# Retention and two feed-forward layers on one core: joining steps, stores, loads and one add put in another order

## The chip, the cores and the metric

The kernel runs on one core of a Trainium2 chip. The metric is the device time of one execution in microseconds. TensorE (PE in the rows) multiplies; VectorE (DVE), ScalarE (ACT) and GpSimd (POOL) do the element work; SyncE (SP) issues nearly all DMAs. The median of three runs is given, and a further execution was profiled.

## The reference

The input is q, k, v in float32, 4 batches of 8 heads, 576 positions, 64 wide, and the weights of two feed-forward layers. What is computed, in float32:

```python
scores = scale * q @ k.T                       # scale = 1/sqrt(64)
ret    = scores * Dmat                         # gamma_h ** (i - j) for i >= j, else 0
x      = (ret @ v), heads side by side         # 2304 x 512
x      = max(x @ w1, x @ w2, x @ w3) @ w_out   # 512 -> 768 -> 512
g, val = x @ w_gate, x @ w_val                 # 512 -> 1536
out    = (g * sigmoid(g) * val) @ w_out2       # 2304 x 512
```

## The kernel before

To keep float32 accuracy a factor is split into two halves (h and l), and a product takes three multiplications: l by h, h by l, h by h. The weights come from memory as 64-bit words (w64) and are joined to float32 by the *joining steps*: ScalarE scales the two words (L115, L121), VectorE shifts and merges them (L123, L124: "wz") and adds (L126: "wl"), ScalarE and GpSimd then split the result (L134 wh, L136 wlo). The order of every engine's instructions is written out by hand: an engine runs its instructions in the order of the program text, so the order of the text is the order of the work.

*Visits.* The retention has 32 units (a pair of heads and half the positions); `visit(n, ...)` handles one: the product with the state and the values (`a_value`, L285 to L292, whose second half xl is L294), the loads for a later unit (`a_load` for kn, vn, L167; `t_load` for qk, eight DMAs at L188), the next state (`a_state`, st, L274), the next scores (`a_score`, pT, L250), and then 4 to 6 *slices* of the first layer. A slice (`f_slice`, L341) is twelve products into one of two PSUM buffers (tag "mm") and one evacuation: for w1 ScalarE copies (L355), for w2 and w3 VectorE takes the maximum (L357). Slices go w1, w2, w3 for each block of 128 hidden columns, each for two halves of 288 tokens (h0, h1). When a maximum is done (w3) it is stored to memory (h_d, L359) by SP. There are three buffers for maxima, so the copy for w1, h1 of a block reuses the buffer of h0 of the block before, and waits for that store to land.

Within a visit the joining steps are divided into shares, one before each slice (L383 to L388). Before unit 16 they join the weights of the first layer; from visit 16 on, `early_steps` (L439) does the same for the second layer's weights: load 512 KB, join, store 256 KB to l_d (L447).

*Remaining slices*, 262 to 339 us: the rest of the first layer; w_out is joined beside it.

*Output stage*, 339 to 417 us (L684): the maxima are loaded back (`h_load`, hf, L524, six buffers, four loads ahead), split (`h_split`, L530 hh on ScalarE, L531 hl), and multiplied with w_out (L698); ScalarE copies the result (L708, "B") and `xsteps` form the operands of the next stage. Beside it `split_parts` (L591) splits the second layer's weights of block 1 and stores them (w_d1, L599), and `split` those of block 0.

*Groups*, from 417 us (L755, index j): the second layer by a scheme with seven products (T1 to T4, B11, B21, B22) in three PSUM buffers g1 to g3. In a group, u (L785) empties g2 before the product "d, T3" may start, p (L797) before "b, T4" may. The add L790 for p5 is on GpSimd, behind GpSimd's gl (L817) of the group before. Between the products `hook()` issues a step of the weights' preparation (`w_steps`, L612 to L627, which need loads of l_d, L431) or of `xsteps`. How many is `pace`.

SP's DMAs land in the order in which they were issued. An instruction that issues a DMA and has to wait holds those behind it on SP.

Of the kernel before, what the change touches and what calls it, by code (L numbers as in the profile page):

```python
# [16 lines left out]
ALU = mybir.AluOpType  # L17
# [51 lines left out]
def retention_moe(ctx, tc, consts, q, k, v, w1, w2, w3, w_out, w_gate, w_val, w_out2, out):  # L69
# [259 lines left out]
    def conv_plan(convs):  # L329

        for _ in range(convs):
            i = wc[0]
            if i < len(win_units):
                wc[0] += 1
                yield (i, 2), (i + 1, 0)
                yield (i, 3), (i + 1, 1)
                yield (i, 4), (i, 5)

    mx = {}

    def f_slice(hb, fi, wi):  # L341
        assert win_units.index((fi, wi)) in ready
        wh, wl = w_in[(fi, wi)]
        cw = TOK[hb][1]
        ps = ps_mm.tile([P, C], F32, name="ps", tag="mm")[:, 0:cw]
        n = 0
        for kc in range(KD):
            xh, xl = xs[(hb, kc)]
            ksl = slice(kc * P, kc * P + P)
            for l, r in ((wh, xl), (wl, xh), (wh, xh)):  # L350
                pe.matmul(ps, l[:, ksl], r, start=n == 0, stop=n == 3 * KD - 1)  # L351
                n += 1
        if wi == 0:
            mx[hb] = ffn.tile([P, C], F32, name="hmax", tag="hmax", bufs=3)[:, 0:cw]
            act.activation(mx[hb], ps, ACTF.Copy)  # L355
        else:
            dve.tensor_tensor(mx[hb], ps, mx[hb], ALU.max)  # L357
        if wi == 2:
            sp.dma_start(out=h_d[hb][fi], in_=mx[hb])  # L359

    fq = []

# [10 lines left out]
            pe.matmul(ps, zero[:, 0:P], zero, start=True, stop=True)  # L373

    def visit(n, slices, convs):
        low = a_value(n)
        if n % 2:
            a_load(n // 2 + 3)
        else:
            t_load(n // 2 + 2)  # L380
        if n % (2 * NP) == 2 * NP - 1:
            fq.extend((n // NP - 1 + h, *w) for w in win_units for h in range(2))
        a_state(n + 1)  # L383
        low()
        a_score(n + 1)
        plan = list(conv_plan(convs))
        done = 0
        for j in range(slices + 1):  # L388
            if j == min(2, slices - 1) or not slices:
                a_prep(n + 2)  # L390
            upto = len(plan) * (j + 1) // (slices + 1)
            for step in plan[done:upto]:
                for i, ph in step:
                    win_phase(i, ph)
            done = upto
            if n >= 16:
                for _ in range(1 if j % 2 else 2):
                    next(early, None)
            if j < slices:
                f_some(1)  # L400

# [134 lines left out]
    for j in range(len(fq) + 1):  # L536
        f_some(1)
        next(steps, None)
        if j % 3 == 0:
            next(steps, None)  # L540
        x = j - late
        if x >= 0 and x % 2 == 0 and x // 2 < F1:
            h_load(0, x // 2)
        if x >= 4 and x % 2 == 0 and (x - 4) // 2 < F1:
            h_split(0, (x - 4) // 2)
    for _ in steps:
        pass
    for fi in range(F1 - 2, F1):
# [42 lines left out]
    def split_parts(fi, nm, src):  # L591

        w = dict(WOPS)[nm]
        for c0 in range(0, w, 256):
            t = xf.tile([P, 2, HT], F32R, name="xt", tag="xt", bufs=3)[:, :, 0:256]
            act.activation(t[:, 0], src[:, c0:c0 + 256], ACTF.Copy)
            yield
            dve.tensor_tensor(t[:, 1], src[:, c0:c0 + 256], f(t[:, 0]), ALU.subtract)
            sp.dma_start(out=w_d[(fi, nm)][:, :, c0:c0 + 256], in_=f(t))  # L599
            yield  # L600

    def w_steps(fis, split=split):

# [75 lines left out]
    xsteps = iter(())  # L679
    NHX = 2 * NBK  # L680
    hq = [(hx, fi) for hx in range(1, NHX) for fi in range(F1)]
    for x in hq[:4]:
        h_load(*x)
    for hx in range(NHX):  # L684
        b, half = divmod(hx, 2)
        if half == 0:
            r = {}
            if b < NBK - 1:
                x_open(b)
        for e in range(KD):  # L690
            ps = ps_mm.tile([P, 512], F32, name="ps2", tag="mm")
            n = 0
            for fi in range(F1):
                wh, wl = wo[fi]
                hh, hl = hsp[(hx, fi)]
                es = slice(e * P, e * P + P)
                for l, rr in ((wh, hl), (wl, hh), (wh, hh)):
                    pe.matmul(ps[:, 0:HT], l[:, es], rr, start=n == 0, stop=n == 3 * F1 - 1)  # L698
                    n += 1
            for fi in ((0, 1), (2,), (), (3, 4, 5))[e]:  # L700
                if hx + 1 < NHX:
                    h_split(*hq.pop(0))
                    if len(hq) > 3:
                        h_load(*hq[3])
            nm = RAW[(e // 2, half)]
            if nm not in r:
                r[nm] = raw(nm)
            act.activation(r[nm][:, e % 2], ps[:, 0:HT], ACTF.Copy)  # L708
            for _ in range(4 if e < 2 else 3):
                next(xsteps, None)  # L710
            if half or hx == 0:
                for _ in range(3):
                    next(steps, None)
        for _ in xsteps:
            pass
        xsteps = (x_second if half else x_first)(b, r)
# [38 lines left out]
    def group(fi, b, hook, lastg=False):  # L755
        X = xop[b]
        g1, g2, g3 = [psg.tile([P, HT], F32, name=f"g{i}", tag=f"g{i}") for i in range(3)]

        def tmp(nm, bufs=1):
            return gw.tile([P, HT], F32, name=nm, tag=nm, bufs=bufs)  # L760

        def prod(ps, w, off, x, first):
            t = wop[(fi, w)]
            xh, xl = X[x]
            n = 0
            for kc in range(2):
                ks = slice(off + kc * P, off + kc * P + P)
                for l, r in ((t[:, 0], xl), (t[:, 1], xh), (t[:, 0], xh)):
                    pe.matmul(ps, l[:, ks], r[:, kc], start=first and n == 0, stop=n == 5, skip_group_check=True)  # L769
                    n += 1  # L770

        def o():
            if pend:
                out2(*pend.pop(0))
            hook()

        prod(g1, "a", 0, "B11", True)
        p1 = tmp("p1", 2)
        act.activation(p1, g1, ACTF.Copy)
        while held:  # L780
            held.pop()()
        hook()
        prod(g2, "c", 256, "T2", True)
        u2 = tmp("u2")
        dve.tensor_tensor(u2, g2, p1, ALU.add)  # L785
        hook()
        prod(g3, "c", 0, "T1", True)
        p5 = tmp("p5", 2)
        act.activation(p5, g3, ACTF.Copy)
        pool.tensor_tensor(p5, p1, p5, ALU.add)  # L790
        hook()
        prod(g1, "a", 256, "B21", False)
        sa = tmp("sa")
        act.activation(sa, g1, ACTF.Sigmoid)
        hook()
        prod(g2, "d", 0, "T3", False)
        dve.tensor_tensor(p5, g2, p5, ALU.add)  # L797
        dve.tensor_tensor(sa, g1, sa, ALU.mult)
        hook()
        o()  # L800
        o()
        prod(g3, "d", 256, "B22", False)
        dve.tensor_tensor(u2, g3, u2, ALU.add)  # L803
        sb = tmp("sb")
        act.activation(sb, u2, ACTF.Sigmoid)  # L805
        hook()
        if not lastg:
            o()
        gh, gl = {}, {}
        for half in (1, 0):  # L810
            for y, t in (("gh", gh), ("gl", gl)):
                t[half] = gw.tile([P, HT], F32R, name=y, tag=y, bufs=8)
            gs[(fi, b, half)] = (gh[half], gl[half])

        def fin(half, t):
            act.activation(gh[half], t, ACTF.Copy)  # L816
            pool.tensor_tensor(gl[half], t, f(gh[half]), ALU.subtract)  # L817

        dve.tensor_tensor(u2, u2, sb, ALU.mult)
        dve.tensor_tensor(p5, u2, p5, ALU.mult)  # L820
        prod(g2, "b", 0, "T4", False)
        fin(1, p5)
        dve.tensor_tensor(p1, g2, p1, ALU.add)
        dve.tensor_tensor(p1, sa, p1, ALU.mult)
        held.append(lambda: fin(0, p1))
        if lastg:
            held.pop()()
        hook()
        if lastg:
            o()  # L830
        if fi % GRP == GRP - 1:
            pend.extend((fi // GRP, b, half, s) for half in (1, 0) for s in range(ROWS))
# [5 lines left out]
    for j, (fi, b) in enumerate(seq):  # L838
# [11 lines left out]
        if (fi, b) == (F2 - 1, 0):  # L850
            for _ in steps:
                pass
        pace = 0 if j == 2 else 2 if j == 3 or fi == F2 - 2 and b == 0 else 1

        def hook():
            beat[0] += 1
            if j < 3 and beat[0] % 2:
                next(xsteps, None)
            for _ in range(pace):
                next(steps, None)  # L860
# [41 lines left out]
```

## Time and profile before

| | us |
|---|---|
| median of three runs | 841.12 (841.1 to 842.18) |
| profiled execution | 842.47 |
| its span, first to last instruction | 840.7 |
| TensorE busy | 816.8 (97%) |
| VectorE busy | 563.0 (67%) |
| ScalarE busy | 315.3 (38%) |
| GpSimd busy | 209.5 (25%) |
| DMA queue of SP, share of 16 engines | 57.4% |
| granted TensorE clock, mean | 1.000 |

An engine's busy time overlaps with that of the others. A number in brackets behind an instruction, such as [2.22 <-DVE hmax L357], is the idle time before it and what ended that. Line numbers in rows are those of the kernel before.

### The profile page before, as it was taken

What the parts mean: (1) busy time and instruction counts of PE and PEld (TensorE: products, weight loads), DVE (VectorE), ACT (ScalarE), POOL (GpSimd) and SP (SyncE); (2) the same over time, 40 slices, a digit from 0 to 9 for tenths busy, and PEclk for the clock granted to TensorE, in tenths of its full rate; (3) what the DMA queues carried; (4) which work ended last, traced back from release to release, by engine and by line L of the source; (5) the groups of instructions that cost most, each with busy time, mean ns of one, the idle gap of its engine ahead of it and who ended that gap; (6) DMA issues with size and microseconds to landing.
All of it is one profiled execution on the core that took longest, in us unless ns stands there. A gap on an engine that the chain in (4) does not pass through costs nothing.

```text
span 840.7 us, 15502 instructions
## 1 busy us (share of the span) xinstructions
PE 816.8 (97%) x5925; PEld 762.4 (91%) x5933; DVE 563.0 (67%) x1004; ACT 315.3 (38%) x633; POOL 209.5 (25%) x197
## 2 busy tenths in 40 slices
PE   8898999999999999999999999999999999999998
PEld 6798888999989999999988999999998999999996
DVE  2668866777775345367578788988989555545555
ACT  2545513333331133446444553444334222332220
POOL 4233430000000002224043223333323333223331
PEclk9999999999999999999999999999999999999999
DMA  9999639999983133675355443443340616665532
GB/s 179 231 208 218 148 73 240 254 245 254 236 233 115 39 127 103 202 210 177 112 233 215 163 153 134 152 150 137 130 149 13 263 39 226 237 217 207 198 105 75
DMA packets 165801, 142.94 MB, mean 170 GB/s; under 512 B 101344, under 2 KB 137952, under 8 KB 165728
## 3 DMA queue, kind: packets, MB, share of 16 engines
q1 hardware_dynamic: 164368, 141.56, 57.4%
q8 instruction: 46, 0.75, 0.4%
q10 hardware_dynamic: 1360, 0.41, 0.2%
q14 instruction: 27, 0.22, 0.1%
HBM read 93.70 MB, written 48.23 MB: 169 GB/s over the span
## 4 chain that ended last, share of the span: by engine, by line
PE 58%; issue 16%; DVE 9%; POOL 7%; DMA 5%; ACT 2%; SPq 2%; POOLq 0%; DVEq 0%; ACTq 0%
PE ps L351 20%; PE g L769 17%; PE ps L746 11%; POOL gl L817 4%; PE ps L698 4%; POOL p L790 2%; PE o_ps L289 2%; PE s L248 2%; DVE wz L124 1%; PE o_ps L285 1%; DMA h_d<-hmax 1%; SPq L188 1%; POOL hl L531 1%; DVE wl L126 1%; DVE wz L123 1%
## 5 line engine op out<-in xcount | busy, mean ns | idle before, releaser
L351 PE MATMUL ps<-xl,wh 128*128 128x288 f32 x576 | 173.5, 301 | 8.7 <-DVE hmax L357 6.4
L351 PE MATMUL ps<-xh,wh 128*128 128x288 f32 x576 | 169.7, 295 | 0.0
L351 PE MATMUL ps<-xh,wlo 128*128 128x288 f32 x576 | 169.6, 294 | 0.0
L817 POOL TENSOR_TENSOR gl<-p,gh 128x384 fp32r<-128x384 f32 x72 | 85.0, 1198 | 275.8 <-ACT gh L816 275.8
L746 PE MATMUL ps<-wp,gh 128*128 128x512 f32 (+1 forms) x436 | 135.3, 391 | 0.4 <-DVE acc L751 0.3
L351 PEld LDWEIGHTS ps<-xl,wh 128*128 128x128 f32 x576 | 108.0, 188 | 13.7 <-DVE hmax L357 6.8
L351 PEld LDWEIGHTS ps<-xh,wlo 128*128 128x128 f32 x576 | 108.1, 188 | 0.0
L351 PEld LDWEIGHTS ps<-xh,wh 128*128 128x128 f32 x576 | 108.1, 188 | 0.0
L746 PEld LDWEIGHTS ps<-wp,gh 128*128 128x128 f32 x436 | 80.7, 188 | 14.4 <-DVE acc L751 1.0
L746 PE MATMUL ps<-wp,gl 128*128 128x512 f32 (+1 forms) x218 | 85.6, 393 | 0.0
L751 DVE TENSOR_TENSOR acc<-ps,acc 128x512 f32<-128x512 f32 (+1 forms) x91 | 62.2, 684 | 33.5 <-PE ps L746 32.3
L357 DVE TENSOR_TENSOR hmax<-ps,hmax 128x288 f32<-128x288 f32 x96 | 43.5, 454 | 60.4 <-PE ps L351 52.4
L769 PE MATMUL g<-xhB,wa 128*128 128x384 f32 x288 | 73.4, 336 | 0.0
L769 PE MATMUL g<-xhT,wc 128*128 128x384 f32 x288 | 73.2, 335 | 0.0
L531 POOL TENSOR_TENSOR hl<-hf,hh 128x384 fp32r<-128x384 f32 x26 | 29.4, 1137 | 132.4 <-ACT hh L530 132.4
L805 ACT ACTIVATE sb<-u 128x384 f32<-128x384 f32 x36 | 18.9, 525 | 112.1 <-DVE u L803 112.1
L816 ACT ACTIVATE gh<-p 128x384 fp32r<-128x384 f32 x72 | 37.8, 525 | 60.8 <-DVE p L820 53.9
L218 POOL TENSOR_TENSOR ks<-kn,cst_a 96x384 f32<-96x384 f32 (+1 forms) x32 | 24.7, 775 | 129.7 <-PE m_ps L264 121.5
L797 DVE TENSOR_TENSOR p<-g,p 128x384 f32<-128x384 f32 x36 | 20.0, 554 | 49.6 <-PE g L769 42.3
L355 ACT ACTIVATE hmax<-ps 128x288 f32<-128x288 f32 x48 | 19.6, 411 | 89.2 <-PE ps L351 77.9
L769 PEld LDWEIGHTS g<-xhB,wa 128*128 128x128 f32 x288 | 52.1, 188 | 0.0
L769 PEld LDWEIGHTS g<-xhT,wc 128*128 128x128 f32 x288 | 52.0, 188 | 0.0
(118 smaller groups left out, 1711.6 us busy)
## 6 DMA issues: line engine op xcount, KB each, us to landing
w<-in_moe_w_out_dram SPq DMA_DIRECT2D x18, 512.0 KB, 4.2
w<-l_d SPq DMA_DIRECT2D x28, 256.0 KB, 3.6
h_d<-hmax SPq DMA_DIRECT2D x48, 144.0 KB, 2.5
w<-in_moe_w_dram SPq DMA_DIRECT2D x12, 512.0 KB, 6.6
w<-in_moe_w_gate_dram SPq DMA_DIRECT2D x12, 512.0 KB, 5.8
w<-in_moe_w_val_dram SPq DMA_DIRECT2D x12, 512.0 KB, 5.4
vn<-in_v_dram SPq DMA_DIRECT2D x16, 288.0 KB, 6.4
out_dram<-acc SPq DMA_DIRECT2D x17, 256.0 KB, 2.0
```

Of the source, the lines that this page charges most:

```text
L218: pool.tensor_tensor(u["ks"][:, 0:nk], u["k"][:, 0:nk], sc, ALU.mult)
L351: pe.matmul(ps, l[:, ksl], r, start=n == 0, stop=n == 3 * KD - 1)
L355: act.activation(mx[hb], ps, ACTF.Copy)
L357: dve.tensor_tensor(mx[hb], ps, mx[hb], ALU.max)
L531: (dve if fi in (3, 5) and hx else pool).tensor_tensor(hl, hf, f(hh), ALU.subtract)
L698: pe.matmul(ps[:, 0:HT], l[:, es], rr, start=n == 0, stop=n == 3 * F1 - 1)
L746: pe.matmul(ps[:, cs], l[:, sl], r[:, cs], start=n == 0, stop=n == 3 * GRP - 1)
L751: dve.tensor_tensor(a[:, cs], ps[:, cs], a[:, cs], ALU.add)
L769: pe.matmul(ps, l[:, ks], r[:, kc], start=first and n == 0, stop=n == 5, skip_group_check=True)
L797: dve.tensor_tensor(p5, g2, p5, ALU.add)
L816: act.activation(gh[half], t, ACTF.Copy)
L817: pool.tensor_tensor(gl[half], t, f(gh[half]), ALU.subtract)
```

## The change

1. In a visit with slices, the first share of joining steps (and, from visit 16 on, the first early steps) is issued right behind `a_value`, ahead of the loads, the state, xl and the scores.
2. A finished maximum is put on a list, and its store is issued at the start of the next slice (`store_mx`), or after the last slice.
3. In the output stage five loads of hf are asked for ahead, not four.
4. `split_parts` gives way once more before it issues a store.
5. The add for p5 is on VectorE for the first three groups, in which GpSimd has no gl that the output waits for.
6. In group 3, `pace` is 1 instead of 2, with one more step per hook from the sixth on; the count of hooks starts anew in each group, and the hooks at which a step of `xsteps` is issued alternate with j.

The code of the change (an instruction at line L of before stands at another line number in the rows of the order of after: L357 at L364, L359 at L345, L447 at L462, L612, L614, L617 at L628, L630, L633, L785 at L801, L790 at L806, L797 at L813, L824 at L840):

```diff
@@ slices @@
     mx = {}
+    done_mx = []
+
+    def store_mx():
+        while done_mx:
+            dst, t = done_mx.pop()
+            sp.dma_start(out=dst, in_=t)
 
     def f_slice(hb, fi, wi):
         assert win_units.index((fi, wi)) in ready
+        store_mx()
...
         if wi == 2:
-            sp.dma_start(out=h_d[hb][fi], in_=mx[hb])
+            done_mx.append((h_d[hb][fi], mx[hb]))
@@ visit @@
     def visit(n, slices, convs):
+        plan = list(conv_plan(convs))
+        done = 0
+
+        def share(j):
+            nonlocal done
+            upto = len(plan) * (j + 1) // (slices + 1)
+            for step in plan[done:upto]:
+                for i, ph in step:
+                    win_phase(i, ph)
+            done = upto
+            if n >= 16:
+                for _ in range(1 if j % 2 else 2):
+                    next(early, None)
+
         low = a_value(n)
+        if slices:
+            share(0)
         if n % 2:
             a_load(n // 2 + 3)
         else:
...
         for j in range(slices + 1):
             if j == min(2, slices - 1) or not slices:
                 a_prep(n + 2)
-            upto = len(plan) * (j + 1) // (slices + 1)
-            for step in plan[done:upto]:
-                for i, ph in step:
-                    win_phase(i, ph)
-            done = upto
-            if n >= 16:
-                for _ in range(1 if j % 2 else 2):
-                    next(early, None)
+            if j or not slices:
+                share(j)
@@ split_parts @@
             dve.tensor_tensor(t[:, 1], src[:, c0:c0 + 256], f(t[:, 0]), ALU.subtract)
+            yield
             sp.dma_start(out=w_d[(fi, nm)][:, :, c0:c0 + 256], in_=f(t))
-            yield
@@ output stage @@
-    for x in hq[:4]:
+    for x in hq[:5]:
         h_load(*x)
...
-                    if len(hq) > 3:
-                        h_load(*hq[3])
+                    if len(hq) > 4:
+                        h_load(*hq[4])
@@ groups @@
-        pool.tensor_tensor(p5, p1, p5, ALU.add)
+        (pool if pend or b == NBK - 1 or fi > 1 else dve).tensor_tensor(p5, p1, p5, ALU.add)
...
-        pace = 0 if j == 2 else 2 if j == 3 or fi == F2 - 2 and b == 0 else 1
+        pace = 0 if j == 2 else 2 if fi == F2 - 2 and b == 0 else 1
+        beat[0] = 0
 
         def hook():
             beat[0] += 1
-            if j < 3 and beat[0] % 2:
+            if j == 3 and beat[0] > 5:
+                next(steps, None)
+            if j < 3 and (beat[0] + j) % 2:
                 next(xsteps, None)
```

TensorE's instructions stand in the same order before and after. Three places show what moves on the other engines.

VectorE in the visit around 83 us; st is the state, xl the second half of the retention's result, pT the scores, hmax the maximum. Before:

```order
L126 ISA wl<-wz,wl 128x1024
L274 SCALAR_TENSOR_TENSOR st<-st,cst_a,m_ps 128x64 x2
L294 TENSOR_TENSOR xl<-o_ps,xh 128x288
L250 TENSOR_TENSOR pT<-s,dm_88 96x576
L123 TENSOR_SCALAR wz<-wz 128x512
L124 SCALAR_TENSOR_TENSOR wz<-w_1053,wz 128x512
L357 TENSOR_TENSOR hmax<-ps,hmax 128x288
```

After:

```order
L126 ISA wl<-wz,wl 128x1024
L123 TENSOR_SCALAR wz<-wz 128x512
L124 SCALAR_TENSOR_TENSOR wz<-w_1053,wz 128x512
L274 SCALAR_TENSOR_TENSOR st<-st,cst_a,m_ps 128x64 x2
L294 TENSOR_TENSOR xl<-o_ps,xh 128x288
L250 TENSOR_TENSOR pT<-s,dm_88 96x576
L364 TENSOR_TENSOR hmax<-ps,hmax 128x288
```

The two merging instructions of the joining moved from behind pT to ahead of the state; the maximum stands behind all of them in both.

SP near 200 us, in a visit of the saturated stretch: h_d are stores of maxima, kn and vn loads of the retention, w loads of weights (512 KB each), l_d stores of joined weights. Before:

```order
L447 DMA l_d_1_106<-w64e 128x512
L359 DMA h_d_59<-hmax 128x288
L167 DMA kn<-in_k_dram 96x12x64
L167 DMA vn<-in_v_dram 96x12x64
L106 DMA w_2865<-in_moe_w_val_dram 128x4x128
L359 DMA h_d_60<-hmax 128x288
L447 DMA l_d_0_107<-wl 128x512
```

After:

```order
L462 DMA l_d_1_106<-w64e 128x512
L106 DMA w_2839<-in_moe_w_val_dram 128x4x128
L167 DMA kn<-in_k_dram 96x12x64
L167 DMA vn<-in_v_dram 96x12x64
L345 DMA h_d_59<-hmax 128x288
L462 DMA l_d_0_107<-wl 128x512
L345 DMA h_d_60<-hmax 128x288
```

The weight load moved ahead of kn and vn, and the first store of a maximum behind all three loads; the second store also stands behind an l_d store now.

VectorE at the start of group j = 3: u and p of the last lines are those of the new group, L824 ends the group before. Before:

```order
L824 TENSOR_TENSOR p_5631<-sa,p_5631 128x384
L612 TENSOR_TENSOR wz<-w_5170 128x256
L614 TENSOR_TENSOR wz<-wz,w_5168 128x256
L785 TENSOR_TENSOR u_5733<-g_5710,p_5718 128x384
L617 TENSOR_TENSOR wz<-w_5168,w_5170 128x256
```

After:

```order
L840 TENSOR_TENSOR p_5631<-sa,p_5631 128x384
L628 TENSOR_TENSOR wz<-w_5173 128x256
L801 TENSOR_TENSOR u_5732<-g_5710,p_5718 128x384
L630 TENSOR_TENSOR wz<-wz,w_5171 128x256
L633 TENSOR_TENSOR wz<-w_5171,w_5173 128x256
```

L614 moved behind u; L612 stays ahead of it.

## Rows read from the trace of the kernel before

**Rows 1.** The page, first part: engine, busy us (share of the span), instructions.

```profile
PE 816.8 (97%) x5925; PEld 762.4 (91%) x5933; DVE 563.0 (67%) x1004; ACT 315.3 (38%) x633; POOL 209.5 (25%) x197
```

**Rows 2.** TensorE's waits: what waited, for what: us in total, times, longest.

```profile
PE ps L351 <- DVE hmax L357: 6.4, 7, 2.2
PE ps L351 <- ACT hmax L355: 2.2, 3, 1.1
PE g L769 <- DVE u L785: 2.0, 2, 1.6
PE g L769 <- DVE p L797: 1.7, 2, 0.9
...
PE ps L698 <- ACT B L708: 1.0, 1, 1.0
...
PE ps L698 <- DVE hl L531: 0.5, 2, 0.3
```

**Rows 3.** Windows: busy us of PE, PEld, DVE, ACT, POOL; clock, DMA share, GB/s.

```profile
140.00:160.00 20.00, 19.77 (x202) 18.67 (x200) 15.54 (x33) 7.13 (x16) 1.20 (x2) 1.00 0.97 250
```

**Rows 4.** Timeline of TensorE: start, duration, instruction, idle before and its end.

```profile
67.49 0.40 PE L351 MATMUL ps<-xl,wh 128*128 128x288 f32 x1 [2.22 <-DVE hmax L357]
...
86.36 0.37 PE L351 MATMUL ps<-xl,wh 128*128 128x288 f32 x1 [1.13 <-DVE hmax L357]
...
131.55 0.40 PE L351 MATMUL ps<-xl,wh 128*128 128x288 f32 x1 [1.07 <-ACT hmax L355]
...
448.55 0.44 PE L769 MATMUL g<-xlT,wd 128*128 128x384 f32 x1 [1.56 <-DVE u L785]
```

**Rows 5.** Timeline of VectorE in the visit around 83 us.

```profile
83.16 0.46 DVE L294 TENSOR_TENSOR xl<-o_ps,xh 128x288 fp32r<-128x288 f32 x1 [0.49 <-ACT xh L292]
...
84.20 0.41 DVE L123 TENSOR_SCALAR wz<-wz 128x512 uint32<-128x512 uint32 x1
84.65 1.20 DVE L124 SCALAR_TENSOR_TENSOR wz<-w,wz 128x512 uint32<-128x512 uint32 x1
85.77 0.44 DVE L357 TENSOR_TENSOR hmax<-ps,hmax 128x288 f32<-128x288 f32 x1
```

**Rows 6.** Timeline of ScalarE, four instructions that waited for DMAs.

```profile
62.57 0.41 ACT L355 ACTIVATE hmax<-ps 128x288 f32<-128x288 f32 x1 [3.29 <-DMA h_d<-hmax]
...
129.98 0.66 ACT L115 ACTIVATE wz<-w 128x512 f32<-128x512 f32 x1 [3.32 <-DMA w<-in_moe_w_gate_dram]
...
222.46 0.41 ACT L355 ACTIVATE hmax<-ps 128x288 f32<-128x288 f32 x1 [4.13 <-DMA h_d<-hmax]
...
370.12 0.52 ACT L530 ACTIVATE hh<-hf 128x384 fp32r<-128x384 f32 x1 [5.05 <-DMA hf<-h_d]
```

**Rows 7.** Timeline of SP: issue, time until the next could be issued.

```profile
203.13 3.21 SPq L106 DMA_DIRECT2D w<-in_moe_w_val_dram  x1
...
365.37 0.54 SPq L524 DMA_DIRECT2D hf<-h_d  x1
...
453.52 1.51 SPq L431 DMA_DIRECT2D w<-l_d  x2
```

**Rows 8.** Chain of waits between 195 and 235 us: start, us, what.

```profile
202.19 8.13 PE ps L351 x60
...
217.81 4.55 DMA h_d<-hmax
```

**Rows 9.** Timeline of VectorE in the first groups.

```profile
431.61 0.56 DVE L797 TENSOR_TENSOR p<-g,p 128x384 f32<-128x384 f32 x1 [0.90 <-POOL p L790]
...
445.64 1.24 DVE L612 TENSOR_TENSOR wz<-w 128x256 f32<-128x256 f32 x1
446.92 1.11 DVE L614 TENSOR_TENSOR wz<-wz,w 128x256 f32<-128x256 f32 x1
...
458.24 0.79 DVE L612 TENSOR_TENSOR wz<-w 128x256 f32<-128x256 f32 x1 [0.38 <-DMA w<-l_d]
```

**Rows 10.** Timeline of GpSimd: the two gl ahead of an add.

```profile
427.62 2.27 POOL L817 TENSOR_TENSOR gl<-p,gh 128x384 fp32r<-128x384 f32 x2 [5.49 <-ACT gh L816]
```

## What the change is expected to do to the time

> **What bounds the kernel now.** Read the page's first part, then the waits of TensorE, then the time windows, then the places. The page says that TensorE is busy for 816.8 us [rows 1]; with a span of 840.7 us some 24 us are left in which it does not multiply, and its work is the same before and after the change. So the question is only which of its waits goes and which new one comes. The waits, grouped by what ended them, are small and few: 6.4 us in seven stalls for a maximum on VectorE, 2.2 us in three for a maximum on ScalarE, 2.0 and 1.7 us in the groups for VectorE's u and p, 1.0 us in the output stage for ScalarE's copy B, 0.5 us there for VectorE's hl [rows 2]. That is 13.8 us, 1.6% of the span, and no edit can give more than what it takes from these rows. The clock is 1.00, its upper level of 2.4 GHz, in the window shown and in the mean of the whole span, so it has no part in the difference. The other resource to look at is the queue of DMAs: at 140 to 160 us its engines are busy 0.97 of the time, with 250 GB/s [rows 3]. A store put behind a load there is late by what the load takes.
>
> **A1, the joining steps ahead of the states.** The longest stalls are 2.22 us, ended at 67.49, and 1.13 us, ended at 86.36 [rows 4]. In both, TensorE's next slice needs the PSUM buffer that a maximum on VectorE has to leave. Around 83 us VectorE shows why: it idles 0.49 us for xh, does xl and pT, then L123 (0.41) and L124 (1.20), and only then the maximum, at 85.77 [rows 5]. The change puts L123 and L124 ahead of the state, xl and pT. Nothing is added or removed on the engine: 1.6 us move past three or four instructions that the maximum waits for as well. So the gain is not 1.6 but the idle time that L123 can fill, 0.49 here, and at most the whole stall, 1.13. For the stall at 67.49 the maximum also follows ScalarE's, which waited 3.29 us for a store to land, until 62.57 [rows 6], and in the new order that store stands behind a 512 KB load (A3): I give that stall no net gain over 0.1. The stalls between 86 and 110 us (of the 6.4, what is left beside these two and three small later ones) have the same form. Value taken: -1.1 us, about 0.5 at each of two visits and 0.1 for the first. Ends: -2.3 (most of the stalls at 67.49 and 86.36 gone) and +0.5 (the idle time fills with nothing, and xl, now later, holds a product).
>
> **A2, loads issued sooner.** At 131.55 TensorE stalls 1.07 us for a maximum on ScalarE [rows 4]. ScalarE was behind its joining copy at 129.98, which had waited 3.32 us for the first w_gate load [rows 6]. In the new order that load no longer stands behind the store of the slice just finished, which the queue can only issue when VectorE is through; it goes out some 1.6 us sooner, about one slice. That exceeds 1.07. Taken: -1.1; ends -1.3 (with a stall of 0.2 us behind the next such load) and 0 (the copy then waits in ScalarE's order for something else).
>
> **A3, the maxima stored one slice later.** This is the edit that can cost. There are three buffers for maxima, so ScalarE's first maximum of a unit's second half takes the buffer of the unit before, and waits until that one's store has landed, three slices on. The row at 222.46 shows the price when it has not: 4.13 us of waiting, for a store issued at 217.81 that took 4.55 us [rows 6, 8]. In the saturated stretch, 140 to 250 us, some stores now have more ahead of them. Near 200 us one goes out just ahead of a load of kn, one of vn, and the w_val load at 203.13 [rows 7]; in the new order it follows all three. So it is issued at about 203.13 + 3.21 = 206.34 and lands, with the 4.55 of the other, near 210.9, or up to 1.4 sooner, by my estimate, since w_val itself now goes out ahead of the state, xl and pT. TensorE runs 60 products, five slices, from 202.19 in 8.13 us [rows 8], 1.63 a slice; the third ends near 207.1, and then ScalarE wants the buffer. TensorE has one other PSUM buffer, so the first 1.6 us of lateness costs nothing: the stall is (209.5 to 210.9) - 207.1 - 1.6 = 0.8 to 2.2 us; and part comes back, since the store at 217.81, which is late today, meets a TensorE that is later. Taken +0.75 here, +0.45 for the two other such stores (near 154 and 228 us), together +1.2; ends 0 (the queue drains) and +3.5.
>
> What the queue does with the order is what decides this. By the row at 217.81 a store took 4.55 us in this stretch [rows 8]. The Trainium skill, "DMA: Bandwidth & Descriptors", section "Queues, rings and completion order", has descriptors consumed in ring order on each DMA engine: by that rule the 1,088 KB of the three loads go first, which at the window's 250 GB/s [rows 3] is 4.4 us by estimate, and A3 would come out at its upper end, the sum at -0.5.
>
> **B, activations loaded five ahead.** In the output stage ScalarE waits 5.05 us for a load of hf, until 370.12 [rows 6]; its copy B is behind that, and TensorE waits for B 1.0 us and for hl 0.5 us [rows 2]. SP issues that load among those at 365.37 [rows 7], behind the first store of a split operand, although six buffers exist and it uses four ahead. With five ahead the load stands before that store in SP's order and needs nothing but a free buffer, which it has, so it goes out a pair of splits earlier. Taken -1.5, all that the two waits hold; ends -1.9 (two small waits for hl more) and -0.5 (the loads that follow are still behind stores, and the wait moves to one of them).
>
> The split stores that move one step later in the same stage cost nothing: the operands are read back only in the groups, and their DMAs lie beside TensorE's products.
>
> **C, the first groups.** TensorE stalls for VectorE's p twice, 1.7 us in all, and for u, 2.0 us in two, of which one stands alone much later and is not touched [rows 2]; the other is the 1.56 us that ended at 448.55 [rows 4]. First p: VectorE waits 0.90 us at 431.61 for GpSimd's add [rows 9], which could start only behind two gl, 427.62 to 429.89 [rows 10]. On VectorE the add costs about what p itself does, 0.56, and the idle 0.90 is filled with it; p comes about 0.5 sooner, so two stalls of 0.85 go to 0.35: -1.0. The add could be longer beside GpSimd's gl: L612, which reads two tiles of SBUF as it does, took 1.24 us at 445.64, beside a gl, and 0.79 at 458.24 [rows 9]; at that ratio the add is 0.88 and the gain nothing. Then u: at 445.64 L612 (1.24) and at 446.92 L614 (1.11) stand ahead of it [rows 9]; the new pace lets only L612 stand there: -1.1. Together -2.1.
>
> That gain is then handed back in part. One group on, VectorE waits for a load of l_d at 458.24 [rows 9] and u is again behind it. That load is issued at 453.52 [rows 7] behind the stores of the operands, which the slower pace makes later, not sooner. In time counted from the start it stays where it is, so TensorE, 2.1 us earlier, waits there for some 1.8. Taken, net: -0.3; ends -2.1 (the load comes sooner too) and +0.4 (the stores, later, push it back).
>
> **The sum.** -1.1 - 1.1 + 1.2 - 1.5 - 0.3 = -2.8 us on the profiled execution (842.47 us: a span of 840.7 and 1.8 around it), that is 839.7. This execution lies 1.35 us above the median of the runs, 841.12, and the difference is taken over: 838.3.
>
> **Rivals.** R1, the groups keep their gain and the queue drains: A3 is 0 and C -2.1: -5.8, 835.3. For it: the load at 453.52 could go sooner with an earlier TensorE, and two buffers of PSUM lie between a late maximum and a stall. Against: the 0.97 of [rows 3] and the 4.55 us of the store at 217.81. R2, only what does not depend on the full queue stays: B alone, and A1 and A2 pay for A3: -1.5 plus 0.4, 840.0; it is for this that L123 and L124 only change places on an engine which has the same work to do before each maximum. R3, slower: the stores of maxima behind loads in the saturated stretch. Place: the three stores near 154, 200 and 228 us. Price: up to 2.2 us each where no state products lie between, about 6.6 together. With A1, A2, B and C as above (-4.0) that is +2.6, 843.7. It decides from 1.6 us of lateness on, beyond one slice. For it speaks the row at 222.46; against it, that TensorE's state products, between visits, cover part. R4, that an edit does not do what it says: the hf loads are held back by their buffers; then B is 0 and the time 839.8, inside the range.
>
> **Chances.** Forecast with its near surroundings (836.5 to 839.8) 0.55; R1 0.15; R2 and R4 0.20; R3 0.10. A measurement of this kernel can tell about 0.2%, 1.7 us, from no change: faster is below 839.4, slower above 842.8. Faster: 0.92 of the forecast, all of R1, a little of R2: 0.69. Slower: most of R3, 0.09. The rest 0.22. Range 835.0 to 841.3: R1 in, R3 out.
>
> **What would show it.** A1: TensorE's waits for hmax on VectorE fall from 6.4 to about 5, with L124 ahead of xl. A2: no stall near 131. A3: ScalarE's waits for h_d grow, with two or three stalls for its maximum near 156, 210 and 230. B: no wait for B near 370. C: the stalls near 431 and 440 shrink to a third, that at 448 to 0.5, and a new one of about 1.8 stands near 457, ended by u. The prediction is wrong if TensorE's busy time or clock moves, if the late stores cost over 3 us, or if the groups keep their 2 us.

## The result: 0.8% slower, and the profile after

The changed kernel takes 849.62 us in the median of six runs (845.74 to 850.22), the kernel before 841.86 in six (841.10 to 844.51): ratio 1.0078, interval 1.0055 to 1.0102. The forecast was 838.3, its range 835.0 to 841.3. The profiled execution of the changed kernel took 847.65 us, with a span of 845.6; its counterpart was 842.47 with 840.7.

TensorE is recorded as busy for 820.8 us against 816.8 [rows 1], as the page's first part for the changed kernel shows. Part of it is that 5933 products have a record here and 5925 before; part is a lower clock, below.

```profile
PE 820.8 (97%) x5933; PEld 764.3 (90%) x5933; DVE 565.0 (67%) x1007; ACT 314.5 (37%) x633; POOL 208.2 (25%) x194
```

TensorE's waits by what ended them, in the changed kernel (us in total, times, longest):

```profile
PE ps L358 <- ACT hmax L362: 5.9, 5, 2.3
PE ps L358 <- DVE hmax L364: 5.1, 6, 1.4
PE g L785 <- DVE u L801: 3.8, 4, 2.0
PE ps L714 <- DVE hl L546: 1.9, 2, 1.6
...
PE g L785 <- DVE p L813: 0.3, 1, 0.3
```

Against [rows 2], the wait for a maximum on VectorE fell from 6.4 to 5.1 and p's from 1.7 to 0.3. But the wait for a maximum on ScalarE rose from 2.2 to 5.9, u's from 2.0 to 3.8, hl's from 0.5 to 1.9.

TensorE's order is the same in both kernels, so the start of the same product can be read in both traces. The difference, after less before:

```
same product, start before   67.5   86.4   95.3  131.6  142.5  145.8  205.4  208.6  227.0
after less before, us       -0.15  -1.45  +0.01  -1.19  -1.69  +0.35  +1.20  +3.74  +2.91
same product, start before  365.2  368.0  371.1  405.8  432.2  438.0  448.6  460.2    end
after less before, us       +4.58  +6.27  +5.32  +3.85  +3.26  +4.27  +2.66  +4.83  +4.94
```

At 142 us the change is 1.7 ahead, although it has lost 1.5 at 95 already. Five steps, that at 95 among them, make the loss, and each is a stall that TensorE did not have. Timeline of TensorE in the changed kernel, the stall in brackets:

```profile
95.31 0.40 PE L358 MATMUL ps<-xl,wh 128*128 128x288 f32 x1 [1.37 <-DVE hmax L364]
...
146.15 0.40 PE L358 MATMUL ps<-xl,wh 128*128 128x288 f32 x1 [2.00 <-ACT hmax L362]
...
212.31 0.40 PE L358 MATMUL ps<-xl,wh 128*128 128x288 f32 x1 [2.26 <-ACT hmax L362]
...
369.80 0.44 PE L714 MATMUL ps<-hl,woh 128*128 128x384 f32 x1 [1.62 <-DVE hl L546]
...
464.98 0.44 PE L785 MATMUL g<-xlT,wd 128*128 128x384 f32 x1 [2.00 <-DVE u L801]
```

The second and third are those of late stores. Timeline of ScalarE in the changed kernel around the first three, with the idle time before the copy of a maximum:

```profile
90.78 0.41 ACT L362 ACTIVATE hmax<-ps 128x288 f32<-128x288 f32 x1 [3.10 <-DMA h_d<-hmax]
...
145.69 0.41 ACT L362 ACTIVATE hmax<-ps 128x288 f32<-128x288 f32 x1 [3.15 <-DMA h_d<-hmax]
...
211.84 0.41 ACT L362 ACTIVATE hmax<-ps 128x288 f32<-128x288 f32 x1 [5.26 <-DMA h_d<-hmax]
```

Before, ScalarE waited three times for a store to land (two of them in [rows 6]), now seven times. Its waits in the two kernels, before first:

```profile
ACT hmax L355 <- DMA h_d<-hmax: 8.7, 3, 4.1
```

```profile
ACT hmax L362 <- DMA h_d<-hmax: 19.8, 7, 5.3
```

The other four in the changed kernel, at 158, 185, 223 and 236 us, have no stall of TensorE behind them. The third of the stores in the rows above in SP's timeline, with what goes out ahead of it (512 KB, then kn, then vn):

```profile
202.09 0.38 SPq L106 DMA_DIRECT2D w<-in_moe_w_val_dram  x1
202.56 0.58 SPq L167 DMA_DIRECT2D kn<-in_k_dram  x1
203.23 2.04 SPq L167 DMA_DIRECT2D vn<-in_v_dram  x1
205.33 3.51 SPq L345 DMA_DIRECT2D h_d<-hmax  x1
```

And the chain of waits of the changed kernel, which passes through all three stores (start, us):

```profile
85.81 4.88 DMA h_d<-hmax
...
138.36 7.22 DMA h_d<-hmax
...
205.33 6.41 DMA h_d<-hmax
```

The store of 205.33 lands at 211.74, when ScalarE has been waiting for 5.26 us.

In the output stage TensorE stalls 1.62 us, ended at 369.80, and then is slow. Windows of the changed kernel around it (busy us of PE, PEld, DVE, ACT, POOL; then granted clock, DMA share, GB/s):

```profile
368.00:370.00 2.00, 0.38 (x3) 0.20 (x2) 2.00 (x4) 0.64 (x2) 1.80 (x2) 1.00 0.11 38
370.00:372.00 2.00, 2.00 (x9) 1.71 (x9) 2.00 (x4) 0.00 (x0) 0.61 (x1) 0.81 0.90 227
372.00:374.00 2.00, 2.00 (x8) 2.00 (x8) 1.59 (x3) 1.32 (x3) 0.00 (x0) 0.50 0.82 242
374.00:376.00 2.00, 2.00 (x11) 2.00 (x11) 1.97 (x2) 0.31 (x1) 1.37 (x1) 0.83 0.61 171
```

From 368 to 370 us TensorE is busy 0.38 us of two. In the next window the granted clock is 0.81 in the mean, then 0.50, which is the lower level of 1.2 GHz, then 0.83. The difference grows from 4.58 to 6.27 us between the stall's end and the clock's return.

### The profile page after: what moved, and what is told of

Its sections match the earlier page's. It is cut to its first block, busy times and chain, and to the rows that moved or that the text cites. A ratio compares the mean times of both kernels' runs of the same rounds, so it can differ in the third digit from the quotient of the medians.

```text
span 845.6 us, 15510 instructions
## 1 busy us (share of the span) xinstructions
PE 820.8 (97%) x5933; PEld 764.3 (90%) x5933; DVE 565.0 (67%) x1007; ACT 314.5 (37%) x633; POOL 208.2 (25%) x194
## 4 chain that ended last, share of the span: by engine, by line
PE 61%; issue 14%; DVE 8%; DMA 6%; POOL 6%; ACT 2%; SPq 2%; POOLq 0%; ACTq 0%; DVEq 0%
PE ps L358 23%; PE g L785 16%; PE ps L762 11%; PE ps L714 4%; POOL gl L833 3%; DMA h_d<-hmax 2%; POOL p L806 2%; PE s L248 2%; PE o_ps L289 2%; PE o_ps L285 2%; DMA kn<-in_k_dram 1%; PE m_ps L264 1%; SPq L188 1%; DVE wl L126 1%; DMA vn<-in_v_dram 1%
## 5 line engine op out<-in xcount | busy, mean ns | idle before, releaser
L364 DVE TENSOR_TENSOR hmax<-ps,hmax 128x288 f32<-128x288 f32 x96 | 43.5, 455 | 68.4 <-PE ps L358 59.9
L785 PE MATMUL g<-xhB,wa 128*128 128x384 f32 x288 | 73.4, 336 | 0.0
L785 PE MATMUL g<-xhT,wc 128*128 128x384 f32 x288 | 73.2, 335 | 0.0
L218 POOL TENSOR_TENSOR ks<-kn,cst_a 96x384 f32<-96x384 f32 (+1 forms) x32 | 26.8, 843 | 131.5 <-PE m_ps L264 123.1
L785 PEld LDWEIGHTS g<-xhB,wa 128*128 128x128 f32 x288 | 52.1, 188 | 0.0
L785 PEld LDWEIGHTS g<-xhT,wc 128*128 128x128 f32 x288 | 52.0, 188 | 0.0
L714 PE MATMUL ps<-hl,woh 128*128 128x384 f32 x144 | 49.3, 342 | 2.0 <-DVE hl L546 1.9
```

Of the source, the lines that this page charges most:

```text
L218: pool.tensor_tensor(u["ks"][:, 0:nk], u["k"][:, 0:nk], sc, ALU.mult)
```

## Experiments

Each was timed beside the kernel before on the same chip, in four groups on four chips: the first four, the next four, the next three, and the last alone. The kernel before took 841.6 to 842.1 us there in the medians, single runs 837.8 to 846.6. Ratios and intervals are within a group and as recorded; they are not exactly the quotients of the medians (for the late stores alone 1.0074, where the medians give 1.0053). Each experiment has one trace, and traces of the same code differ: the three kernels that leave the visits as they were (five ahead, the groups' part, the groups' part mended) are 0.2 to 1.1 us behind the trace of before at 260 us.

**Stores at once.** The change without its deferred stores:

```diff
         if wi == 2:
-            done_mx.append((h_d[hb][fi], mx[hb]))
+            sp.dma_start(out=h_d[hb][fi], in_=mx[hb])
```

> The change without its second part: every maximum is stored at once, as before. Theory A (the late stores put SP's store behind weight and kn/vn loads, ScalarE then waits for its landing, and TensorE stalls near 94, 144 and 210 us): those three stalls (1.4, 2.0 and 2.7 us) go, TensorE is about 1 us ahead of the kernel before at 260 us instead of 2.9 behind, and the time falls from about 849 to 844-845; the rest of the loss, in the output stage and the groups, stays. Rival B (not the late stores but the weight loads, which the joining steps now issue ahead of kn and vn, make SP late): the stalls near 144 and 210 stay and the time is above 847.

840.21 us, ratio 0.9991 (0.9973 to 1.0008), level with the kernel before; the expected gain was exceeded. TensorE is 3.5 us ahead at 227 us where the change is 2.9 behind, and its waits there are:

```profile
PE ps L351 <- DVE hmax L357: 3.4, 4, 1.2
PE ps L351 <- ACT hmax L355: 2.2, 3, 1.3
```

Without the late stores the whole loss in the time is gone. Rival B falls: the weight loads stand ahead of kn and vn here as well.

**Only the late stores**, on the kernel before (the `slices` part of the diff, with the store after the last slice).

> The kernel before with only the stores of the maxima one slice later. Theory A: ScalarE waits longer for h_d, TensorE is 1 to 3 us later at 260 us, time 842.5 to 845. Rival B: without the joining steps ahead of the loads the stores lie behind less, no stall is added, 841 to 842.

846.06 us, ratio 1.0074 (1.0052 to 1.0096), above what theory A expected. TensorE stalls for ScalarE's maximum:

```profile
PE ps L358 <- ACT hmax L362: 5.6, 4, 2.9
PE ps L358 <- DVE hmax L364: 4.3, 3, 2.2
```

The stalls are at 144.7 (1.62 us) and 209.3 (2.90). At 131 us this kernel gains the 1.23 us that A2 was to gain. Not all of its trace's loss of 2.3 us is the stores': the clock is at 0.50 for 3.41 us from 67.6 on, at the end of a stall of 2.23 us that the kernel before has there too (2.22 [rows 4], with no fall behind it), which is 1.7 us by itself.

**Only the activations five ahead**, with the split stores one step later.

> The kernel before with only the activations loaded five ahead and the split stores one step later. Theory C (the fifth load pushes the loads of l_d behind it by about 1 us; the split operands and hl are late with them, TensorE stalls once for hl near 365 us for about 1.6 us, and the granted clock falls to 0.5 for some 3.5 us): the stall and the low clock are there, TensorE leaves the output stage about 1 us later than before, time 842 to 843.5. Rival D (the stall near 368 came only from what the visits had done before it): no stall, no low clock, time 839.5 to 840.5.

841.58 us, ratio 1.0015 (0.9995 to 1.0034). In the trace the wait for B is gone, no stall for hl over 0.3 us is there, and no low clock; TensorE gains about 1.1 us in the stage. Theory C fails for this part alone, and its rival D is right about the trace but not about the time: the median of twelve runs shows no gain. That the wait for B went by this edit is not shown either, since it is gone as well in two kernels that leave the stage alone (below, with the combination).

**Only the groups' part** (add on VectorE, pace, hooks).

> The kernel before with only the add on VectorE and the new pace in the first groups. Theory E (the two stalls for p shrink by 0.5 each, but xl of an operand now stands ahead of u in the third group, and the l_d load of group 4 is later, which costs 2 us there): 0 to 1 us more than before, 841.5 to 842.5. Rival F (the loss of the groups came from SP being late in the whole program): the groups gain 1 to 2 us, 839.5 to 840.5.

843.93 us, ratio 1.0023 (1.0003 to 1.0044), more than theory E expected, whose mechanism is in the trace: the stalls for p shrink to 0.31 and less than 0.25, and two new ones come. Timeline of TensorE in this kernel:

```profile
437.50 0.45 PE L769 MATMUL g<-xlT,wd 128*128 128x384 f32 x1 [0.95 <-DVE u L785]
...
460.19 0.45 PE L769 MATMUL g<-xlT,wd 128*128 128x384 f32 x1 [2.01 <-DVE u L785]
```

From 428 us to 460 us it loses 1.06 us, in the change 1.05.

**Only the joining steps ahead.** The `visit` hunks of the diff alone.

> The kernel before with only the joining steps of the first share ahead of the states (and so the weight loads ahead of kn and vn). Theory A (this part gains what the forecast gave A1 and A2, and more): the stalls near 65, 85 and 130 us shrink, TensorE is 2 to 3 us ahead at 260 us, time 839 to 840 where before has 841.6. Rival B (the gain seen with the stores at once belongs to the other parts): within 0.5 us of before at 260 us.

838.69 us, ratio 0.9960 (0.9938 to 0.9982): theory A, but for the stall near 130, which stays (1.14 us). TensorE is 3.2 us ahead at 260 us. Its waits in this kernel:

```profile
PE ps L351 <- DVE hmax L357: 3.9, 4, 1.2
...
PE ps L351 <- ACT hmax L355: 1.6, 2, 1.1
```

**Late stores of the second halves alone**, in the whole change:

```diff
-            done_mx.append((h_d[hb][fi], mx[hb]))
+            if hb % 2:
+                done_mx.append((h_d[hb][fi], mx[hb]))
+            else:
+                sp.dma_start(out=h_d[hb][fi], in_=mx[hb])
```

> The whole change, but only the maxima of the second halves are stored one slice later; those of the first halves at once. Theory A (the harm comes from the first halves' stores, for whose buffers ScalarE waits three slices on; a second half's buffer is wanted two slices later than that): the stalls near 94, 144 and 208 us are gone and TensorE is about 3 us ahead at 260 us, as with every store at once; time 840 to 841. Rival G (any late store delays the next ones on SP by filling the queue): half of the 6 us is left, 843 to 846.

839.02 us, ratio 0.9977 (0.9954 to 1.0000). TensorE is 6.2 us ahead at 227 us, more than theory A expected, and no stall near 94, 144 or 208 is left. The harm comes from the first halves' stores; rival G falls.

**The groups' part mended**, on the kernel before: the add and the pace, hooks as before, and

```diff
             yield from split(fi, "b", a22)
+            ask(NO + 3 * fi + 4)
             yield from split(fi, "c", sc)
```

> The groups' part alone on the kernel before, with two things undone or added: the hooks at which a step of the operands is issued stay as before, and the loads of l_d for the next block are asked for right behind the split of b, ahead of the stores of c and d. Theory E (the loss of the groups is the late load at group 4, 2.2 us, and xl ahead of u in the third group, 1.0): both stalls are gone, the gain of 2 us stays to the end, 839.5 to 840. Rival H (VectorE is full in these groups, and another of its steps takes the place): the stall at group 4 shrinks by less than 1 us, 841 to 842.5.

839.09 us, ratio 0.9967 (0.9946 to 0.9988). SP's timeline in this kernel has the loads of l_d between the stores of b and c:

```profile
448.70 0.32 SPq L589 DMA_DIRECT2D w_d2b<-wb  x1
449.08 1.45 SPq L431 DMA_DIRECT2D w<-l_d  x2
450.93 0.32 SPq L589 DMA_DIRECT2D w_d2c<-wc  x1
```

The stall in the third group is gone. That at group 4 is half of what it was, and VectorE no longer waits there for a load; what holds u are its own steps, so rival H holds here (the stall shrinks by 0.95 us), though the time is theory E's:

```profile
457.39 0.45 PE L770 MATMUL g<-xlT,wd 128*128 128x384 f32 x1 [1.06 <-DVE u L786]
```

From 428 to 460 us this kernel gains 0.9 us. The added line also runs in the output stage, where `w_steps` prepares blocks 0 and 1, and there this trace gains 2.6 us, so this is not an experiment on the groups alone.

**The combination**: joining steps ahead, stores at once, five ahead, the mended groups.

> All that helps together: joining steps ahead of the states, every maximum stored at once, activations five ahead, the add on VectorE, the pace with the hooks as before, the loads of l_d ahead of two stores. By the sum of theories A, C, E: -3 in the visits, -1.5 in the output stage, -2 in the groups, 835 to 836 where before has 841.6. If rival H or the stall for hl near 362 stays: 837.5 to 839.

835.78 us, ratio 0.9929 (0.9905 to 0.9953). Its trace is of the slowest of its eleven runs (839.39), with stalls of 1.00, 1.34 and 1.36 us at 204, 223 and 253. In the output stage L612 (here L620) runs without a wait for its load, and hl without a stall of TensorE. Timeline of VectorE in this kernel:

```profile
359.24 0.42 DVE L620 TENSOR_TENSOR wz<-w 128x256 f32<-128x256 f32 x1
...
362.57 0.56 DVE L539 TENSOR_TENSOR hl<-hf,hh 128x384 fp32r<-128x384 f32 x1 [0.30 <-ACT hh L538]
```

How long TensorE is in the output stage (us, one trace each, between the products that start at 339.0 and 417.0 in the trace of before) shows which edit does this:

```
stage as before           before 78.0, late stores alone 77.6, groups' part 76.0, joining steps alone 75.9
five ahead                alone 76.9, stores at once 77.3, late second halves 77.8, four buffers 77.8,
                          the change 79.1 (1.7 of it the low clock) and 77.4 (second trace)
l_d asked for sooner      without five ahead (groups mended) 75.4; with it 75.4 (combination), 75.4 and 75.5 (the two best)
```

The sooner l_d loads give 75.4 to 75.5 with and without five ahead. That five ahead helps is not shown: the stage takes 75.9 to 78.0 without it and 76.9 to 77.8 with it, at full clock.

**Four buffers for maxima**, in the whole change:

```diff
-            mx[hb] = ffn.tile([P, C], F32, name="hmax", tag="hmax", bufs=3)[:, 0:cw]
+            mx[hb] = ffn.tile([P, C], F32, name="hmax", tag="hmax", bufs=4)[:, 0:cw]
```

> The whole change with four buffers for maxima instead of three. Theory A (what hurts is ScalarE's wait for the buffer whose store has not landed): with a fourth buffer the wait falls away for as long as one more slice, the stalls near 94, 144 and 208 us go although every store is still late, time 839 to 842. Rival I (the late stores hurt by what they push back on SP, loads of weights and of kn and vn): the visits still lose 3 us or more against the kernel with stores at once, 845 or more.

837.54 us, ratio 0.9961 (0.9938 to 0.9984). One buffer takes back 12 us, with every store as late as before. TensorE's waits in this kernel:

```profile
PE g L785 <- DVE u L801: 3.8, 4, 2.0
PE ps L358 <- DVE hmax L364: 2.2, 3, 1.2
PE ps L714 <- DVE hl L546: 1.9, 2, 1.6
...
PE ps L358 <- ACT hmax L362: 0.5, 1, 0.5
```

The one wait for ScalarE's maximum that is left, 0.5 us, stands in the kernel before too (at 167.20). No copy of a maximum waits over 0.3 us for a store any more. Rival I falls.

**The change again**, unchanged, on this chip.

> The whole change as it is, on this chip, for a second trace. Theory A: stalls near 94, 144 and 208 us as before, time 847 to 850. Where its clock falls below 1.00 it does so right after one of its stalls of 1.5 us or more, though not after each; if no such fall shows, the difference of some 2 us between its runs is not the clock's.

849.42 us, ratio 1.0089 (1.0057 to 1.0121). In this trace the clock stays at 1.00, with stalls of 1.98 us at 142 and 3.07 at 207, and the execution takes 844.65. It is the one run with a mean of 1.000, so the trace cannot tell whether the clock makes the difference between the runs. Its seven runs by their mean clock, beside others of the same group:

```
mean clock           1.000          0.998    0.996            0.994            0.990
the change           844.65         847.09   849.32, 849.42   849.85, 851.29   855.40
kernel before        841.23 (of 9)  842.50 (of 3)
four buffers         836.2 (of 2)   837.9 (of 8)   842.86      843.87
```

The difference between its runs goes with the clock, some 2 us for each 0.002. Of the 7.7 us between the two medians of this group, 3.4 are there at a clock of 1.000 (844.65 against 841.23), and 4.2 go with the clock. The split is rough: 844.65 is a single run, and the nine of the kernel before spread from 838.08 to 844.99 at that clock. By the same table the fourth buffer is worth 8.5 us at 1.000 and the rest of its 12 by the clock.

**Best.** The combination, with the second halves' stores late.

> The combination of all that helped, with the second halves' maxima stored one slice later and the first halves' at once. If the visits of the kernel with half of the stores late, 6 us ahead at 260 us, add to the mended output stage and groups: 833 to 835, and no stall above 1.2 us but the one near 456. If the late stores of the second halves gained nothing and the 3 us were that run's luck: 835.5 to 837, as the combination with stores at once.

835.45 us, ratio 0.9917 (0.9896 to 0.9938), between the two cases and level with the combination. Its trace is the first case's: TensorE is 5.0 us ahead at 227 us, and no stall is above 1.2.

**Best with four buffers**, every store late.

> The best combination with four buffers for maxima and every store one slice later. Theory A: with the fourth buffer no store has to be at once, so this stands level with the best combination, 834 to 836; its clock is at 1.00 in most runs, since no stall of 1.5 us is left. Rival I (late stores still push other transfers back): 837 or more.

833.40 us, ratio 0.9903 (0.9880 to 0.9925): 1.0% faster than the kernel before, and all six runs at a clock of 1.000. That it beats the best with three buffers is not shown (the intervals overlap); rival I falls here too. TensorE's waits in this kernel:

```profile
PE ps L358 <- DVE hmax L364: 2.0, 2, 1.2
PE g L786 <- DVE u L802: 1.9, 3, 1.1
...
PE ps L358 <- ACT hmax L362: 0.5, 1, 0.5
```

## Why the prediction was wrong

The step that failed is A3, the price of the late stores: taken at +1.2 us, with +3.5 as its end. In the trace the steps at 95, 146 and 209 us are +1.46, +2.05 and +2.53, together +6.0. (The step at 205, +0.85, is not shown to be the stores': the combination, with every store at once, stalls 1.00 us at 204 too.) Against the kernel with the stores at once, which differs in nothing else, the change is 6.4 us later at 260 us, and 4.9 in the second trace of the change. The mechanism was the one described, and R3, which is the same mechanism at its full price, was given 0.10. That R3's 6.6 us come near is partly luck, for two of its three places do not stall.

- *Which stores.* Of the places named, 154, 200 and 228 us, only 200 stalls. At the other two ScalarE waits, 2.71 us until 158.19 and 1.70 until 235.94, and TensorE does not, as it has its second buffer. Those at 85.81 and 138.36 were not looked at. The first costs in a second way: ScalarE, held until 90.78, is late with the state, and with it VectorE and the next visit's maximum, so TensorE stalls at 94 (1.37 us) and A1's gain there is gone.
- *How late.* The store near 200 us was to land between 209.5 and 210.9 and cost 0.8 to 2.2 us, and I took 0.75, below that range, for a part that was to come back. At 227 us 0.82 does come back, but with the joining steps alone 0.78 does too. The store was issued at 205.33, about as worked out, and took 6.41 us, not the 4.55 of its model in [rows 8]; that at 138.36 took 7.22. Its stall of 2.26 us is the upper end. It landed at 211.74, behind the vn ahead of it (211.39). Here the trace agrees with the Trainium skill's ring order ("DMA: Bandwidth & Descriptors", "Queues, rings and completion order"), by which A3 was to come out at its upper end; the two places left out took it beyond.

A1 was right and too small. With A2 it was -2.2; alone it ran 3.0 us faster. Timeline of VectorE in the changed kernel, in the visit of [rows 5]:

```profile
80.83 0.42 DVE L123 TENSOR_SCALAR wz<-wz 128x512 uint32<-128x512 uint32 x1
81.28 0.69 DVE L124 SCALAR_TENSOR_TENSOR wz<-w,wz 128x512 uint32<-128x512 uint32 x1
81.89 0.59 DVE L274 SCALAR_TENSOR_TENSOR st<-st,cst_a,m_ps 128x64 f32<-128x64 f32 x2
82.40 0.45 DVE L294 TENSOR_TENSOR xl<-o_ps,xh 128x288 fp32r<-128x288 f32 x1
82.76 0.74 DVE L250 TENSOR_TENSOR pT<-s,dm 96x576 f32<-96x576 f32 x1
83.53 0.46 DVE L364 TENSOR_TENSOR hmax<-ps,hmax 128x288 f32<-128x288 f32 x1
```

The maximum starts at 83.53 and not at 85.77, 2.24 us sooner: the idle 0.49 is gone; L124 takes 0.69 there, not 1.20; and the row of steps starts 1.25 sooner, out of the visit before, where L235 takes 0.46 and not 1.57. Both longer times of before began beside an instruction of GpSimd that had already started, which the sum of A1 did not look at; in the changed kernel VectorE started first. Timeline of GpSimd in the kernel before:

```profile
78.16 1.30 POOL L136 TENSOR_TENSOR wlo<-wl,wh 128x512 fp32r<-128x512 f32 x1 [2.77 <-ACT wh L134]
...
84.17 1.13 POOL L218 TENSOR_TENSOR ks<-kn,cst_a 96x384 f32<-96x384 f32 x1
```

The whole stall of 1.13 us goes, and not 0.5 of it. How much of the stall of 2.22 at 67.49 goes by A1 is not shown: it is 0.91 to 2.23 us in the traces that leave the joining steps as they were.

A2 was right in size, 1.19 us at 131, but it belongs to the late stores: with them alone it is there, with the joining steps alone a stall of 1.14 us remains.

B was to give 1.5 us; the stage costs 0.9 in the change, with 1.7 for the low clock in it, and gains 0.6 in the second trace, at full clock. The sum took a wait of one trace for one of the kernel: ScalarE's 5.05 us for hf is 2.6 and 2.5 with the groups' part alone and the joining steps alone, and TensorE does not wait for B there. What I gave as its other end, a wait that moves on, is what happened, and to the loads of l_d. Timeline of VectorE in the changed kernel:

```profile
365.76 0.42 DVE L628 TENSOR_TENSOR wz<-w 128x256 f32<-128x256 f32 x1 [3.94 <-DMA w<-l_d]
...
368.40 2.63 DVE L546 TENSOR_TENSOR hl<-hf,hh 128x384 fp32r<-128x384 f32 x2
```

L612 (here L628) waits 3.94 us for its load, 2.91 before, and the two hl behind it need 2.63 us. The combination, with these loads ahead of two stores, has neither. In the five traces that have both the joining steps and five ahead, without these sooner loads, L612 waits 3.6 to 4.0 us and TensorE stalls 1.3 to 1.6 us for hl. In those with only one of the two, or neither, it waits 2.4 to 3.1 us, and that stall is not there. That the stores one step later in the split were free was not tried apart.

C was right about p (1.7 to 0.3) and had the handed-back gain right in place and a little too small. The late load was to give back 1.8 us at group 4; it is 2.00 (the row at 464.98). What I did not see is the shift of the hooks by j: it puts an xl, L650 (here L666), ahead of u in the third group. Timeline of VectorE in the changed kernel:

```profile
440.00 1.77 DVE L666 TENSOR_TENSOR xt<-t,xt 128x768 fp32r<-128x768 f32 x1
...
463.61 0.85 DVE L628 TENSOR_TENSOR wz<-w 128x256 f32<-128x256 f32 x1 [1.26 <-DMA w<-l_d]
```

That is 0.95 us of stall at 442. A further 0.59 us, for ScalarE's p at 449.46, takes back half of what u gains in group 3 (0.43 left of 1.56); the mended groups, with the hooks as before, have neither. Net +1.0 instead of -0.3.

The clock was left out: "it has no part in the difference". It is 1.00 in the trace of before, and was taken to stay so for any order. In the change's trace it costs 1.7 us after a stall; by its runs beside one another on another chip, a little over half of the loss, as far as one run at 1.000 tells.

R1 and R2 fall with A3. R4 falls in its condition, since ScalarE's wait for hf near 370 is gone in every trace with five ahead; its worth for B, nothing, is not refuted.

## What to carry to other kernels

Before a store is put off, list for each reuse of its buffer the time between landing and need, and add what is put ahead of it on the queue; a store whose buffer is wanted soon stays at once, or gets one buffer more (12 us here for 1,152 bytes a partition). Moving one load ahead on a queue is not free for the next: five hf loads ahead, with the joining steps ahead too, made the l_d loads late, and moving those as well took that back. A wait read from one trace is to be priced only if it comes again in a second one: the wait for B was 1.0 us in the trace of before and nothing in two others of the same stage. In a kernel that keeps TensorE busy, a new stall of a microsecond or two is to be priced with a chance of the lower clock behind it.

## What the runs showed of the hardware

- The granted clock fell to 0.50 right after a stall in some executions and not in others with the same stall: after 1.62 us here, and not after 3.07 and 2.01 in the second trace of the change, nor after the same 1.62 with four buffers (at 360.00). The combination, whose longest stall is 1.36 us, held a mean of 1.000 in 10 of 11 runs, the two best, with 1.2, in 4 and 6 of six; the change held it in one of seven, the kernel before in 9 of 18 beside it.
- VectorE and GpSimd slow each other. The two hl of the change on VectorE took 2.63 us while GpSimd's two ran beside them (2.41 from 368.20 on; one alone took 1.01 at 360.26); the same two of VectorE took 1.01 us before (at 364.56). The four together took 2.83 us, nearly what they take one behind the other, 3.0. The xl at 440.00 took 1.77 us beside two gl, others of its shape 0.94. The Trainium skill, "SBUF — State Buffer", "Who interferes with whom", gives an exclusive lock for such pairs, with which these numbers agree; the add, moved to VectorE, took 0.89 us in that place and 0.56 elsewhere.
